# Storing the last group's two larger chunks in two transfers each, in a 1x1 depthwise-separable convolution

## The chip, the cores and the metric

The kernel runs on one core of one Trainium2 chip. The metric is the device time of one execution in microseconds (us), as the median of several runs. A profiled run also gives the span: the time from the first to the last of the program's own instructions, some 1.7 us shorter than the device time here.

The **tail** is the time from the end of the last matmul to the end of the span, and the **head** is what lies before the kernel's steady pitch begins. The last matmul's end is read from the trace's record of that instruction.

## The reference

The kernel size is 1, so the depthwise step is a scale of each channel and the whole thing is one matrix product with a scaled weight.

```python
H = W = 384; C = 384; k = 1
x  : (1, H, W, C) bf16     dw : (1, 1, C) bf16     pw : (C, C) bf16

def reference(x, dw, pw):
    ...                       # for k = 1: out = x * dw[0, 0]
    return jnp.einsum('bhwc,cd->bhwd', out, pw)
```

147,456 rows of 384 channels go in and as many come out: 113 MB each way.

## The kernel before

The rows are cut into 288 supertiles of 512 rows. For each, VectorE transposes the input (two instructions), TensorE multiplies it with the scaled weight (48 matmuls into one of two halves of PSUM), and ScalarE copies the result from PSUM into an output buffer in one instruction. SyncE issues all stores and nearly all loads. Supertiles are loaded and stored in chunks; the chunks are small at both ends (comments in the code cuts are this document's; an assert is cut):

```python
NR = 3          # input and output buffers, used in turn by the groups
def _groups(n_super):
    head, tail = [[1, 1, 2, 2, 4]], [[6, 4], [4, 2, 1, 1]]
    mid = n_super - sum(map(sum, head + tail))
    return head + [[LMAX]] * (mid // LMAX) + tail      # LMAX = 10
```

So the last group is four supertiles in one chunk, two in one chunk, and two single ones. A store waits until the chunk's last supertile has been emptied out of PSUM:

```python
def store(t):
    g, i, off, first, L = chunks[t]
    je = first + L - 1
    src = Os[g % NR][:, 4 * off * D : 4 * (off + L) * D]
    rows = of[512 * first : 512 * (first + L), :]
    if first + LONG < NS:                  # all but the last two supertiles
        dst = rows.rearrange("(q p j) d -> p q (j d)", q=4, p=P)
        src = src.rearrange("p (q e) -> p q e", q=4)
    else:
        dst = rows.rearrange("(m q) d -> m (q d)", q=4)
    if je + 1 == NS:                       # the last supertile: two halves
        for k in range(2):
            part = slice(2 * D * k, 2 * D * k + 2 * D)
            nc.sync.wait_ge(s_a[je % 2], je // 2 + 2 + k)
            nc.sync.wait_ge(s_d, k + 1)
            nc.sync.dma_start(dst[:, part], src[:, part]).then_inc(s_o[g % NR], 16)
        return
    nc.sync.wait_ge(s_a[je % 2], je // 2 + 2)
    nc.sync.dma_start(dst, src).then_inc(s_o[g % NR], 16)
```

The last supertile alone is emptied by ScalarE and VectorE together, a quarter each in turn, so that its first half can be stored earlier:

```python
for q in (0, 2):
    nc.scalar.copy(Ov[:, q, j, :], PS[s][:, q, :D]).then_inc(s_a[s])
    nc.vector.tensor_copy(Ov[:, q + 1, j, :], PS[s][:, q + 1, :D]).then_inc(s_d)
```

At the very end SyncE waits until all stores have landed.

## Time and profile before

| | before |
|---|---|
| median of the first 3 runs | 575.23 us (575.2 to 575.54) |
| span of the profiled run | 573.9 us |
| TensorE busy, share of the span | 567.8 us, 99% |
| VectorE, ScalarE busy | 89%, 73% |
| data moved | 226.88 MB, 395 GB/s |
| end of the last matmul | 569.24 us |
| tail | 4.63 us |

The prediction below shows the lines.

### The profile page before, as it was taken

The page shows a single profiled execution, that of the slowest core. Times are in us where ns is not written, and L with a number is a line of the kernel's source. Part 1 is how long each engine was busy: PE and PEld are TensorE (multiplying, and loading weights), DVE is VectorE, ACT ScalarE, POOL GpSimd, SP SyncE. Part 2 cuts the span into 40 slices and gives each one's busy share as a digit, 9 for nine tenths or more (in the row PEclk, how much of TensorE's full clock was granted, in tenths as well). Part 3 has the DMA queues.
Part 4 walks back from the last instruction along what each step waited for, and adds up shares of the span by engine and source line. Part 5 has one row for each costly group of instructions (what it writes and reads, how often), then busy time and mean ns, then how long its engine had stood idle before and what let it go on. Part 6 is the DMA issues. An engine that isn't in the chain of part 4 may idle for free.

```text
span 573.9 us, 29721 instructions
## 1 busy us (share of the span) xinstructions
PE 567.8 (99%) x13869; PEld 383.5 (67%) x13869; DVE 508.0 (89%) x584; ACT 419.1 (73%) x297; POOL 0.9 (0%) x8
## 2 busy tenths in 40 slices
PE   8999999999999999999999999999999999999996
PEld 4666666666666666666666666666666666666664
DVE  7888988988898898889889888988988898898884
ACT  6777777777777777777777777777777777777775
POOL 0000000000000000000000000000000000000000
PEclk9999999999999999999999999999999999999999
DMA  8999999999999999999999999999999999999676
GB/s 358 441 340 422 427 417 435 430 432 421 412 404 414 389 393 418 407 399 397 435 390 399 398 427 399 393 414 417 403 390 430 400 389 397 419 403 369 266 286 234
DMA packets 25396, 226.88 MB, mean 395 GB/s; under 512 B 1193, under 2 KB 5418, under 8 KB 21546
## 3 DMA queue, kind: packets, MB, share of 16 engines
q1 hardware_dynamic: 24208, 225.61, 97.1%
q10 hardware_dynamic: 1178, 1.18, 0.6%
q14 instruction: 9, 0.07, 0.0%
q8 instruction: 1, 0.02, 0.0%
HBM read 113.54 MB, written 113.25 MB: 395 GB/s over the span
## 4 chain that ended last, share of the span: by engine, by line
PE 99%; DVE 0%; issue 0%; POOL 0%; POOLq 0%; DVEq 0%; SPq 0%
PE ps L189 98%; PE ps L239 1%; PE ps L206 0%; DVE O L330 0%; POOL zero L255 0%; POOL warm L254 0%; PE ps L221 0%; POOLq L365 0%; DVEq L326 0%; SPq L103 0%
## 5 line engine op out<-in xcount | busy, mean ns | idle before, releaser
L189 PE MATMUL ps<-w_r,T 32*128 32x384 bf16 x13824 | 562.2, 321 | 0.0
L282 DVE STREAM_TRANSPOSE T<-X 128x384 uint32<-128x384 uint32 x572 | 501.2, 877 | 55.4 <-DMA X<-in_x_dram 0.2
L332 ACT CAST O<-ps 128x1536 bf16<-128x1536 f32 x287 | 413.0, 1439 | 147.5 <-PE ps L189 147.5
L189 PEld LDWEIGHTS ps<-w_r,T 32*128 32x128 bf16 x13824 | 381.5, 93 | 181.0 <-issue 0.7
L295 ACT CAST w_r<-ps 128x768 bf16<-128x768 f32 x5 | 3.7, 805 | 1.1 <-PE ps L239 1.0
L206 PE MATMUL ps<-zero 32*128 32x384 bf16 x24 | 2.6, 494 | 1.4 <-POOL zero L255 1.4
L282 DVE STREAM_TRANSPOSE T<-Xl 128x384 uint32<-128x384 uint32 x4 | 3.5, 878 | 0.4
L330 DVE CAST O<-ps 128x384 bf16<-128x384 f32 x2 | 1.0, 553 | 3.1 <-PE ps L189 3.1
L239 PE MATMUL ps<-pw_n,sel_w 64*128 64x384 bf16 x18 | 3.1, 521 | 0.0
L267 ACT ACT_TABLE_LOAD x1 | 1.3, 1283 | 1.9 <-issue 1.9
L206 PEld LDWEIGHTS ps<-zero 32*128 32x128 bf16 x24 | 0.7, 99 | 2.6 <-issue 2.6
L239 PEld LDWEIGHTS ps<-pw_n,sel_w 64*128 64x128 bf16 x18 | 1.2, 139 | 1.5 <-issue 1.2
L300 DVE TENSOR_REDUCE sel<-eye 128x64 f32<-128x128 bf16 x1 | 0.3, 289 | 1.8 <-POOL eye L257 1.8
L295 DVE CAST w_r<-ps 128x768 bf16<-128x768 f32 x1 | 1.0, 957 | 0.9 <-PE ps L239 0.9
L329 ACT CAST O<-ps 128x384 bf16<-128x384 f32 x2 | 0.9, 482 | 0.5 <-PE ps L189 0.5
L310 DVE TENSOR_SCALAR sel_w<-sel,dw_f 128x256 bf16<-128x256 f32 x3 | 0.9, 351 | 0.0
L307 DVE COPY dw_f<-ps 128x3 f32<-128x3 f32 x1 | 0.2, 161 | 0.8 <-PE ps L221 0.8
L221 PEld LDWEIGHTS ps<-ones,dw_row 1*128 1x128 bf16 x3 | 0.2, 101 | 0.2 <-issue 0.2
L257 POOL TENSOR_SCALAR_AFFINE_SELECT eye<-ones 128x128 bf16<-128x128 bf16 x1 | 0.3, 295 | 0.1
L267 ACT COPY warm<-warm 128x1 f32<-128x1 f32 x2 | 0.3, 190 | 0.0
L255 POOL MEMSET zero<- 128x192 uint32 x1 | 0.3, 258 | 0.0
L221 PE MATMUL ps<-ones,dw_row 1*128 1x1 bf16 x3 | 0.2, 161 | 0.0
(6 smaller groups left out, 0.7 us busy)
## 6 DMA issues: line engine op xcount, KB each, us to landing
X<-in_x_dram SPq DMA_DIRECT2D x26, 3840.0 KB, 21.0
out_dram<-O SPq DMA_DIRECT2D x26, 3840.0 KB, 26.8
X<-in_x_dram SPq DMA_DIRECT2D x3, 1536.0 KB, 17.0
out_dram<-O SPq DMA_DIRECT2D x3, 1536.0 KB, 6.9
X<-in_x_dram SPq DMA_DIRECT2D x3, 768.0 KB, 8.3
out_dram<-O SPq DMA_DIRECT2D x3, 768.0 KB, 14.3
X<-in_x_dram SPq DMA_DIRECT2D x1, 2304.0 KB, 18.6
out_dram<-O SPq DMA_DIRECT2D x1, 2304.0 KB, 10.5
```

The lines of the kernel that those rows point to most:

```text
L189: mm = nc.tensor.matmul(PS[s][:, q, :D], lhsT=Ts[s][32 * q : 32 * q + 32, b, par::2], rhs=w_r[32 * q : 32 * q + 32, b, par, :], start=(b, ...
L206: nc.tensor.matmul(PS[0][:, i, :D], lhsT=zero[32 * i : 32 * i + 32, 0:P], rhs=zero[32 * i : 32 * i + 32, :], start=True, stop=True, tile_p ...
L221: mm = nc.tensor.matmul(PS[1][:, 0, D + k : D + k + 1], lhsT=dw_row[:, P * k : P * k + P], rhs=ones[0:1, 0:1], start=True, stop=True,)
L239: mm = nc.tensor.matmul(PS[(k + 1) % 2][:, 2 * r + v, :D], lhsT=sel_w[64 * v : 64 * v + 64, k, r, :, :].rearrange("p q w -> p (q w)"), rhs ...
L255: nc.gpsimd.memset(zero[:].bitcast(U32), 0).then_inc(s_zero)
L267: c = nc.scalar.copy(warm[:, s + 1 : s + 2], warm[:, 0:1])
L282: ins = nc.vector.transpose(out=Tw[:, 3 * h : 3 * h + 3], in_=Xw[:, :, j, 96 * h : 96 * h + 96].rearrange("p k (b w) -> p b k w", w=32),)
L295: o = nc.vector.tensor_copy(out, in_) if e == 0 else nc.scalar.copy(out, in_)
L310: nc.vector.tensor_scalar_mul(sel_w[:, k], sel[:].unsqueeze(2).to_broadcast([P, 2, 4, 32]), dw_f[:, k : k + 1]).then_inc(s_sw)
L329: nc.scalar.copy(Ov[:, q, j, :], PS[s][:, q, :D]).then_inc(s_a[s])
L330: nc.vector.tensor_copy(Ov[:, q + 1, j, :], PS[s][:, q + 1, :D]).then_inc(s_d)
L332: a = nc.scalar.copy(Ov[:, :, j, :], PS[s][:, :, :D])
```

## The change

Its intent is to start the last group's big stores earlier, so that they don't stand in front of the small last ones. The chunks of four and of two are each stored in two transfers, each issued when its part has been emptied.

```diff
+    n_parts = [2 if c[0] + 1 == len(groups) and (c[4] > 1 or c[3] + 1 == NS) else 1 for c in chunks]
...
-        def store(t):
-            je = first + L - 1
+        def store(t, k):
+            je = first + L * (k + 1) // n_parts[t] - 1
...
                 src = src.rearrange("p (q e) -> p q e", q=4)
+                e = L * D // n_parts[t]
+                dst, src = dst[:, :, e * k : e * k + e], src[:, :, e * k : e * k + e]
...
-            todo.append((first + L + 1, store, t))
+            for k in range(n_parts[t]):
+                todo.append((first + L * (k + 1) // n_parts[t] + 1, store, (t, k)))
...
-            n = sum(map(len, groups[o::NR])) + ((len(groups) - 1) % NR == o)
+            n = sum(n_parts[t] for t, c in enumerate(chunks) if c[0] % NR == o)
```

Cut: the last supertile's two halves take the new argument `k` in place of their own loop, and do what they did; `todo` holds tuples of arguments.

More of the change, by code (lines that the diff above doesn't have):

```diff
@@ L133, in store @@
                 src = src.rearrange("p (q e) -> p q e", q=4)
+                e = L * D // n_parts[t]
+                dst, src = dst[:, :, e * k : e * k + e], src[:, :, e * k : e * k + e]
             else:
                 dst = rows.rearrange("(m q) d -> m (q d)", q=4)
-            if je + 1 == NS:
-                for k in range(2):
-                    part = slice(2 * D * k, 2 * D * k + 2 * D)
-                    nc.sync.wait_ge(s_a[je % 2], je // 2 + 2 + k)
-                    nc.sync.wait_ge(s_d, k + 1)
-                    nc.sync.dma_start(dst[:, part], src[:, part]).then_inc(s_o[g % NR], 16)
+            if first + 1 == NS:
+                je = first
+                part = slice(2 * D * k, 2 * D * k + 2 * D)
+                nc.sync.wait_ge(s_a[je % 2], je // 2 + 2 + k)
+                nc.sync.wait_ge(s_d, k + 1)
+                nc.sync.dma_start(dst[:, part], src[:, part]).then_inc(s_o[g % NR], 16)
                 return
@@ L153 @@
             if 0 < t < NT - LONG:
-                todo.append((g_end[g - NR] if g >= NR else -1, load_x, t))
-            todo.append((first + L + 1, store, t))
-        for _, f, t in sorted(todo, key=lambda a: a[0]):
-            if f is store and t == 0:
+                todo.append((g_end[g - NR] if g >= NR else -1, load_x, (t,)))
+            for k in range(n_parts[t]):
+                todo.append((first + L * (k + 1) // n_parts[t] + 1, store, (t, k)))
+        for _, f, a in sorted(todo, key=lambda a: a[0]):
+            if f is store and a[0] == 0:
                 for _ in range(28):
                     nc.sync.wait_ge(s_pw, 16)
-            f(t)
+            f(*a)
         for o in range(NR):
-            n = sum(map(len, groups[o::NR])) + ((len(groups) - 1) % NR == o)
+            n = sum(n_parts[t] for t, c in enumerate(chunks) if c[0] % NR == o)
             nc.sync.wait_ge(s_o[o], 16 * n)
```

## The prediction

> **What bounds the kernel now.** I read the page's busy shares first, then the chain of work that ended last, then the end of the span microsecond by microsecond, then the store queue's timeline and its packets. The chain, in order of time:
>
> ```profile
> 7.05 562.22 PE ps L189 x13824
> 569.26 0.03 issue
> 569.29 0.02 DVEq L326
> 569.31 0.04 issue
> 569.36 1.02 DVE O L330 x2
> ```
>
> TensorE alone sets the time from 7.05 us to 569.26 us: 13,824 matmuls back to back, 98% of the span. The granted clock is 1.00 all the way. The change touches no matmul, so at most what lies behind 569.26 us can move. The span ends at 573.86 us (573.9 on the page), so that is 4.6 us, 0.8% of the time.
>
> What fills these 4.6 us? The chain stops at 570.38 us, with the last copy out of PSUM; what follows is transfers, which the chain doesn't follow. The table by stage, one row a microsecond (columns: PE, weight load, VectorE, ScalarE, GpSimd busy, clock, DMA share, GB/s):
>
> ```profile
> 562.00:563.00 1.00, 1.00 (x32) 0.68 (x28) 0.90 (x2) 0.93 (x1) 0.00 (x0) 1.00 0.00 0
> 563.00:564.00 1.00, 1.00 (x32) 0.66 (x24) 0.90 (x2) 0.56 (x1) 0.00 (x0) 1.00 0.16 61
> 564.00:565.00 1.00, 1.00 (x33) 0.66 (x25) 0.90 (x2) 0.88 (x1) 0.00 (x0) 1.00 1.01 402
> ...
> 570.00:571.00 1.00, 0.00 (x0) 0.00 (x0) 0.38 (x1) 0.15 (x1) 0.00 (x0) 1.00 1.00 390
> 571.00:572.00 1.00, 0.00 (x0) 0.00 (x0) 0.00 (x0) 0.00 (x0) 0.00 (x0) 1.00 1.01 367
> 572.00:573.00 1.00, 0.00 (x0) 0.00 (x0) 0.00 (x0) 0.00 (x0) 0.00 (x0) 1.00 0.05 15
> ```
>
> The DMA engines move nothing in 562 to 563 us and are then full, without a hole, until just after 572 us. So the tail has a backlog of stores that begins late. Who begins it is seen in the store queue's timeline (start, length, line; read in single stretches):
>
> ```profile
> 555.15 0.37 SPq L144 DMA_DIRECT2D out_dram<-O  x1
> 562.95 0.37 SPq L144 DMA_DIRECT2D out_dram<-O  x1
> 566.85 2.29 SPq L144 DMA_DIRECT2D out_dram<-O  x2
> 568.80 0.34 SPq L144 DMA_DIRECT2D out_dram<-O  x1
> 570.00 0.85 SPq L141 DMA_DIRECT2D out_dram<-O  x2
> ```
>
> These are the stores of the group before's last chunk (4 supertiles), then of the last group: 4 supertiles (1536 KB), 2 (768 KB, at 566.85), 1 (384 KB, at 568.80) and the last one in two halves of 192 KB (570.00 and 570.46). With 1.573 + 0.786 + 0.393 + 0.393 = 3.146 MB at some 380 GB/s they need 8.3 us, and by the packet records they run from 563.85 to 572.16 us. The last store lands at 572.54 us, SyncE's wait for it ends at 572.56 us, and 1.30 us of closing semaphores and drains follow to 573.86 us.
>
> **What the Trainium skill says, and whether the trace agrees.** (1) DMA: Bandwidth & Descriptors, section "Queues, rings and completion order": on each DMA engine descriptors are consumed in ring order. The trace agrees: the first 1536-byte packet of the 2-supertile store starts at 567.85 us, just as the 3072-byte packets of the store before run out (567.97 us), though it was issued at 566.85. A late big store thus delays the small last ones. (2) Same page, "Latency and other measured facts": first byte some 600 ns after issue on the sync and scalar path. The trace differs: where the engines had room, the first packet came 0.90 us after the issue's start (547.35 to 548.25, 555.15 to 556.05, 562.95 to 563.85); I use 0.90. (3) Same page, "Anatomy of one DMA": a fixed cost of about 2 us, mostly the receipt of the write. Stated for GpSimd's path; the last two stores here took 2.0 and 2.1 us with 0.53 us of packets in each, and from the last packet's end to the landing it is 0.38 us only. (4) Same page, "Why small descriptors are slow (HBM only)": each packet has a small fixed overhead. The trace lets it be measured, below.
>
> **The change part by part.** It removes no byte and adds two store issues: the 4-supertile store becomes two of 768 KB, issued after its second and its fourth supertile is emptied; the 2-supertile store becomes two of 384 KB. The instruction lists of TensorE, VectorE, ScalarE and GpSimd stay the same.
>
> *Issue times.* One copy out of PSUM ends each supertile, every 1.95 us:
>
> ```profile
> 557.59 1.44 ACT L332 CAST O<-ps 128x1536 bf16<-128x1536 f32 x1 [0.51 <-PE ps L189]
> 559.54 1.44 ACT L332 CAST O<-ps 128x1536 bf16<-128x1536 f32 x1 [0.51 <-PE ps L189]
> 561.49 1.44 ACT L332 CAST O<-ps 128x1536 bf16<-128x1536 f32 x1 [0.51 <-PE ps L189]
> ```
>
> The store at 562.95 follows the copy that ends at 562.93, so 561.49 is the chunk's fourth supertile and 557.59 its second. Part A of the four can go at 559.05, part B stays at 562.95. Of the two, part A goes at 562.95 + 1.95 = 564.90 and part B stays at 566.85. SyncE sits idle at both new times; an issue takes it 0.37 us.
>
> *Packet times.* 128 partitions over 16 engines are 8 packets an engine for each contiguous piece. The share of queue 1 in 564.2 to 567.6 us (3072-byte packets only) and in 568.2 to 569.8 us (1536-byte only), and of queue 10 in 34 to 38 us (768-byte packets of another transfer):
>
> ```profile
> q1 hardware_dynamic: 440, 1.35, 102.8%
> ...
> q1 hardware_dynamic: 384, 0.59, 101.6%
> ...
> q10 hardware_dynamic: 225, 0.17, 12.7%
> ```
>
> 3.4 us x 16 x 1.028 / 440 = 127 ns; 1.6 x 16 x 1.016 / 384 = 68 ns; 4 x 16 x 0.127 / 225 = 36 ns. That is about 6 ns a packet plus 0.039 ns a byte. Four supertiles whole: 32 packets x 127 ns = 4.06 us; in halves 2 x 32 x 67 ns = 4.29 us. Two supertiles whole: 32 x 67 = 2.14 us; in halves 2 x 32 x 36 = 2.30 us. The split costs 0.39 us of DMA time in all, but 2.14 us of it is moved into the hole before 563.85 us.
>
> *The queue replayed.* A part starts at its issue + 0.90 us or when the part before it is through:
> - 4A: 559.95, but the chunk before holds 15 engines until 560.17 and one, which lags, until 561.50. Through at 562.3, on the laggard at about 563.7: before 4B in both cases.
> - 4B: 563.85 to 565.99. 2A: ready 565.80, so 565.99 to 567.14.
> - 2B: 567.75 to 568.90: here the backlog is gone for the first time.
> - Single supertile: 569.70, 8 x 127 ns, to 570.72. Last supertile, first half: 570.90 to 571.43 (8 x 67 ns). Second half: ready 571.36, so 571.43 to 571.97.
>
> Check on before: the same rule gives 563.85 + 4.06 + 2.14 + 1.02 + 0.54 + 0.54 = 572.15, against 572.16 in the records. So the last packet ends 0.2 us earlier, and landing and closing follow unchanged: the span should be about 573.66 us. Without a hole for the last half, the limit is that its data is there only at 570.46 us: 0.90 + 0.54 + 0.38 later is 572.28 us, so 0.26 us is all the gain that these latencies leave, whatever is done to the earlier stores. Median 575.23 - 0.2 = 575.0 us. That is 0.04%, far below the 2% mark.
>
> **The rivals.**
> - *The issue latency takes the backlog's place, but is smaller.* The stores of the last two supertiles have one contiguous piece a partition, not four. Both were hidden behind the backlog, so 0.90 us is shown only for the four-piece form. With the skill's 0.6 us the last landing would be at 570.46 + 0.6 + 0.54 + 0.38 = 571.98, a gain of 0.56 us: 574.7 us. Against it: a load at the start with one piece a partition, issued at 1.54 us, first moved at 2.95 us, no sooner than the stores[...].
> - *The split eats its own gain.* If packets of 768 bytes in a store cost more than the 36 ns read off a load, 2B has 0.80 us of slack before the single supertile (568.90 to 569.70), so up to 61 ns a packet stays hidden. If descriptors came too slowly or the laggard engine held 4A past 563.85, 4B could start later, by a few tenths. Then the gain is 0 to 0.1 us: 575.2 us.
> - *The transfer is hidden anyway.* If the closing waited for something else, nothing would move. SyncE's wait for the stores ended 0.02 us after the last landing, which speaks against it: chance small.
> - *TensorE gets slower* as stores lie beside matmuls from 560 to 562 us. Stores lie beside them now (564 to 569 us) with the same 32 matmuls a microsecond. Nothing.
>
> **Range and chances.** The gain has a middle of 0.2 us and lies between 0 and 0.56 us by the rivals. The three runs of before lie 0.34 us apart (575.2 to 575.54), as large as the gain, and a median of such runs moves by some 0.15 us. Low: 575.2 - 0.56 is 574.64, so 574.6. High: no gain and a median 0.2 us up, 575.4. A difference of 2% is 11.5 us, more than twice what lies behind the last matmul, so faster by 2% could not come from the change; slower by 2% would need TensorE to stall. 0.99 for within 2%.
>
> **What would show it right or wrong.** In the changed trace: store issues at 559.05 and 564.90 besides the old ones; DMA share near full in 560.2 to 562.3 us; 4B still first moving at 563.85 us; 768-byte packets of 36 ns; a first hole in the DMA share between about 568.9 and 569.7 us; the last packet's end near 572.0 and the landing near 572.33 us; the last half 1.9 us from issue to landing in place of 2.08. Wrong would be: no hole before the single supertile (then packet cost), or the single store's packets starting less than 0.90 us after 568.80 (then the first rival), or a chain whose matmuls end at another time than 569.26 us.

## The result, and the profile after

The changed kernel took 575.19 us in the median of 6 runs (575.01 to 575.78); the kernel before, in 6 runs that include the first three, 575.29 us (575.15 to 575.81). The ratio is the mean time of one kernel's fast runs over that of the other's of the same rounds, so it isn't quite the ratio of these medians: 0.9998, with a 95% interval of 0.9985 to 1.0011.

The span of the profiled run fell from 573.9 to 573.3 us, 0.59 us, more than the medians did. Two stages made that, and only one has to do with the change.

**The head.** The first copy of a supertile out of PSUM, in the timelines of ScalarE, before and then after (start, length, line; in brackets the idle time before it):

```profile
9.64 1.44 ACT L332 CAST O<-ps 128x1536 bf16<-128x1536 f32 x1 [1.33 <-PE ps L189]
```

```profile
9.15 1.44 ACT L336 CAST O<-ps 128x1536 bf16<-128x1536 f32 x1 [0.92 <-PE ps L193]
```

It comes 0.48 us earlier after, and by the records so do all 289 of ScalarE's copies, each by 0.481 or 0.482 us: both kernels keep a pitch of 1.95 us from the first supertile to the last. So 0.48 of the 0.59 us were won before 10 us, where both programs are the same. The stage of the product's first matmuls says how (TensorE alone; columns: busy with the number of matmuls, clock, DMA share, GB/s), before and then after:

```profile
7.00:8.00 1.00, 0.95 (x16) 1.00 1.02 412
8.00:9.00 1.00, 1.00 (x32) 1.00 1.03 424
```

```profile
7.00:8.00 1.00, 1.00 (x28) 1.00 1.01 418
8.00:9.00 1.00, 1.00 (x32) 1.00 1.01 418
```

The full rate is 32 matmuls a microsecond. Before, the first twelve ran at about half of it: in the records the groups of four start 0.27 to 0.32 us apart and then 0.163 us. After, they start 0.163 to 0.173 us apart from the first group on. The matmuls that fold the scale into the weight, just before, show the same halving: their pairs start 0.32 us apart and then 0.163 us, from 5.6 us on after, and not at all before. The three slow groups cost 0.42 us, and the product's first matmul began 0.07 us later as well. The Trainium skill has it: TensorE: Matmul & The Clock Gate, section "What's actually happening", says that the array starts at half clock, that a short window of activity releases it, and that this window runs freely, so that the point of release differs from run to run. The trace agrees in the factor of two and in the scatter (below), though the clock column shows 1.00 throughout. This difference belongs to the run, not to the kernel.

**The tail.** It fell from 4.63 to 4.52 us, by 0.11 us. The store queue's timeline of the changed kernel, read in single stretches:

```profile
558.57 0.37 SPq L147 DMA_DIRECT2D out_dram<-O  x1
562.47 0.37 SPq L147 DMA_DIRECT2D out_dram<-O  x1
564.42 0.37 SPq L147 DMA_DIRECT2D out_dram<-O  x1
566.37 0.37 SPq L147 DMA_DIRECT2D out_dram<-O  x1
568.32 0.34 SPq L147 DMA_DIRECT2D out_dram<-O  x1
569.52 0.82 SPq L144 DMA_DIRECT2D out_dram<-O  x2
```

All old issues stand where they stood, 0.48 us earlier (562.95 is now 562.47, 570.00 is 569.52), and the new ones at 558.57 and 564.42 are 0.48 us before the predicted 559.05 and 564.90. The stages of the changed kernel, with the columns of the prediction's table:

```profile
559.00:560.00 1.00, 1.00 (x35) 0.74 (x28) 0.88 (x1) 0.94 (x1) 0.00 (x0) 1.00 1.00 363
560.00:561.00 1.00, 1.00 (x32) 0.74 (x28) 0.88 (x1) 0.49 (x1) 0.00 (x0) 1.00 1.01 370
561.00:562.00 1.00, 1.00 (x32) 0.74 (x28) 0.90 (x2) 0.99 (x1) 0.00 (x0) 1.00 0.76 267
...
568.00:569.00 1.00, 0.76 (x20) 0.28 (x12) 0.13 (x1) 0.49 (x2) 0.00 (x0) 1.00 0.51 167
569.00:570.00 1.00, 0.00 (x0) 0.00 (x0) 0.90 (x2) 0.66 (x2) 0.00 (x0) 1.00 0.85 335
570.00:571.00 1.00, 0.00 (x0) 0.00 (x0) 0.00 (x0) 0.00 (x0) 0.00 (x0) 1.00 0.79 286
571.00:572.00 1.00, 0.00 (x0) 0.00 (x0) 0.00 (x0) 0.00 (x0) 0.00 (x0) 1.00 0.46 166
```

The idle stretch of before is now full up to 561.8 us, and the DMA share has holes after 568 us, where before it was 1.00 until 572 us. The backlog is gone. What the last two stores gained by it is small; the line for their way from issue to landing, before and then after:

```profile
DMA to landing us min/median/max: 2.0/2.0/2.1
```

```profile
DMA to landing us min/median/max: 1.9/1.9/2.0
```

By the records the last one took 2.08 us before and 1.97 us after, and these 0.11 us are the whole of the tail's change.

**A trap in the page.** The chain of the changed kernel ends like this:

```profile
564.88 0.02 issue
564.90 1.45 ACT O L336
566.35 0.02 issue
566.37 2.51 DMA out_dram<-O
568.88 1.01 DVE O L334 x2
```

It says that VectorE's last copies waited for the landing of a store, and TensorE's share falls from 98% to 97% by it. That is not so. VectorE does check that semaphore, but for the stores of earlier groups in the same buffer, which had long landed. The semaphore is shared with the new part, whose landing happened to come close to the moment when the copy began, and the inference took it for the releaser. VectorE's copy starts 0.12 us after the end of the last matmul in both kernels, so TensorE released it in both. By the records the last of the new part's 16 increments came 0.23 us after that matmul, when the copy had begun already.

### The profile page after: what moved, and what is told of

Read it like the earlier page. It is cut to its first block, busy times and chain, and to the rows that moved or that the text cites. A ratio compares the mean times of both kernels' runs of the same rounds, so it can differ in the third digit from the quotient of the medians.

```text
span 573.3 us, 29723 instructions
## 1 busy us (share of the span) xinstructions
PE 566.7 (99%) x13869; PEld 411.9 (72%) x13869; DVE 507.4 (89%) x584; ACT 419.0 (73%) x297; POOL 0.9 (0%) x8
## 4 chain that ended last, share of the span: by engine, by line
PE 97%; DMA 1%; ACT 1%; DVE 0%; issue 0%; SPq 0%
PE ps L193 97%; DMA pw_n<-in_pw_dram 1%; DMA out_dram<-O 0%; ACT w_r L299 0%; ACT O L336 0%; DVE O L334 0%; PE ps L243 0%; SPq L369 0%; SPq L104 0%
## 5 line engine op out<-in xcount | busy, mean ns | idle before, releaser
L193 PE MATMUL ps<-w_r,T 32*128 32x384 bf16 x13824 | 561.8, 321 | 0.5 <-ACT w_r L299 0.5
L193 PEld LDWEIGHTS ps<-w_r,T 32*128 32x128 bf16 x13824 | 410.0, 93 | 152.3 <-issue 0.9
```

What stands on the lines that cost most here:

```text
L193: mm = nc.tensor.matmul(PS[s][:, q, :D], lhsT=Ts[s][32 * q : 32 * q + 32, b, par::2], rhs=w_r[32 * q : 32 * q + 32, b, par, :], start=(b, ...
```

## The experiments

Eight runs were made, six of them of new kernels, all but two with correct results. Since the head scatters by more than the effect, they are judged by the tail. Single runs on one core have the state "unknown"; times are compared only in the two cases that ran in several rounds.

**1. Both kernels once more: `rep_before` and `rep_after`** (no edit). How well does a tail repeat?

> The kernel before once more, to learn how well a profile repeats. The tail (from the end of the last matmul to the end of the span) was 4.63 us before and 4.52 us after the change; the head (up to where the copies out of PSUM settle at a pitch of 1.95 us) differed by 0.48 us the other way round of what the change could do. If the tail is set by the stores as I think, it comes out at 4.63 +- 0.03 us again, while the span may differ by some 0.5 us. If the tail scatters by 0.1 us too, the change's 0.11 us is not shown by one profile.

> The changed kernel once more. If the 0.11 us of tail is the change's own, the tail is 4.52 +- 0.03 us again; if it was scatter, it may come out near 4.63 us. The head is expected to differ from run to run whatever the kernel.

Measured: tails of 4.63 us (`rep_before`) and 4.52 us (`rep_after`), as in the first pair. Tails repeat to 0.01 us, so 0.11 us is clear of scatter. The spans went the other way: 573.6 us for the kernel before and 573.9 us for the changed one. The reason is in the head again: against the first profile of before, the copies came 0.32 us earlier in `rep_before` and 0.14 us later in `rep_after`. Over all ten profiles that shift covers 0.76 us, seven times the change's effect. Two things make it, by the records: the matmuls reach their full rate between 5.6 us (`after`) and 8.2 us (`six3`), which costs the product's first groups up to 0.5 us, and the first matmul on the loaded weight starts between 3.96 and 4.21 us. A comparison of medians could not have shown the 0.11 us.

**2. One split at a time: `only4` and `only2`.**

```diff
-    ... (c[4] > 1 or c[3] + 1 == NS) ...
+    ... (c[4] == 4 or c[3] + 1 == NS) ...     # only4
+    ... (c[4] == 2 or c[3] + 1 == NS) ...     # only2
```

> Only the four-supertile chunk is stored in two parts; the two-supertile chunk goes whole. Replay, in us from the end of the last matmul: second part of the four done at -3.1, the chunk of two (issued -2.39) moves from -1.49 to 0.78, the single supertile to 1.80, the halves of the last to 2.34 and 2.88 on the engine that is last. So the last packet ends at 2.88, against 2.92 before and 2.81 after: tail about 4.59 us. If instead moving the four's first half into the idle stretch is all that counts, the tail equals the changed kernel's, 4.52.

> Only the two-supertile chunk is stored in two parts; the four goes whole and late as before. Replay: the four moves from -5.4 to -1.2, the halves of the two follow with 32 packets of 38 ns each, to 1.2, the single to 2.2, the last halves to 2.8 and 3.3. So the last packet ends near 3.2 us against 2.92 before: tail about 4.9 us, 0.25 us longer than before. If any split of a late store helps by itself, the tail is at or below 4.63 us.

Measured: tails of 4.55 us and of 4.95 us. For `only4` that is neither the expected 4.59 us nor the 4.52 us of the alternative: the chunk of four alone wins 0.08 of the 0.11 us. The replay was right in kind: the single supertile's packets start 0.64 us after the last matmul, just as those of the chunk of two run out, where with both splits they start at 0.40 us. Its last packet came at 2.85 us, 0.03 us sooner than replayed. The chunk of two alone loses 0.31 us against before. The last two stores of `only2` from issue to landing:

```profile
DMA to landing us min/median/max: 2.3/2.4/2.4
```

Splitting a store that stands in a full queue only adds packets: in `only2` the 768-byte packets took 39 ns each, so that 64 of them an engine last 2.5 us where 32 of 1536 bytes last 2.1 us. In these runs a split helps by what it moves into idle time; a gain of another kind does not show.

**3. The size of the backlog: `six1` and `six3`.** The last group's chunks are 6, 1 and 1, and the six is stored whole, or in three parts.

```diff
-    ... tail = [[1, 1, 2, 2, 4]], [[6, 4], [4, 2, 1, 1]]
+    ... tail = [[1, 1, 2, 2, 4]], [[6, 4], [6, 1, 1]]
-    n_parts = [2 if c[0] + 1 == len(groups) and (c[4] > 1 or c[3] + 1 == NS) else 1 for c in chunks]
+    n_parts = [1 if c[0] + 1 == len(groups) and c[4] == 6 else 2 if c[3] + 1 == NS else 1 for c in chunks]   # six1
+    n_parts = [3 if c[0] + 1 == len(groups) and c[4] == 6 else 2 if c[3] + 1 == NS else 1 for c in chunks]   # six3
```

> The last group's chunks are 6, 1 and 1 and the six is stored whole, at -2.39 us. If the backlog of late stores sets the end, 32 packets of 184 ns run from -1.49 to 4.4 us, the single to 5.4, the last halves to 6.5 us: tail about 8.2 us, 3.6 us longer than before, and the median some 3.6 us over before's (0.6%). If the end is set by the last store's own latency and the stores before it are hidden, the tail stays at 4.6 us.

> Chunks 6, 1 and 1 with the six stored in three parts of two supertiles, each when emptied. From the parts on this is the same queue as the kernel that splits the four alone: last packet near 2.88 us, tail 4.59 us (+- 0.05), so that the split is worth 3.6 us here where it is worth 0.1 us in the change. If splitting itself had a gain or a cost of its own, it would show here as a tail off 4.59 us.

Measured: tails of 8.14 us and of 4.51 us. The times, in 4 runs each: 578.76 us (578.69 to 578.81) for `six1`, a ratio of 1.0061 to before (1.0044 to 1.0078), and 575.23 us for `six3`, a ratio of 0.9998 (0.9981 to 1.0015). In `six1` the stages after the last matmul (at 568.93 us) are full of transfer:

```profile
572.00:573.00 1.00, 0.00 (x0) 0.00 (x0) 0.00 (x0) 0.00 (x0) 0.00 (x0) 1.00 1.00 401
573.00:574.00 1.00, 0.00 (x0) 0.00 (x0) 0.00 (x0) 0.00 (x0) 0.00 (x0) 0.67 1.02 399
574.00:575.00 1.00, 0.00 (x0) 0.00 (x0) 0.00 (x0) 0.00 (x0) 0.00 (x0) 0.50 1.01 366
575.00:576.00 1.00, 0.00 (x0) 0.00 (x0) 0.00 (x0) 0.00 (x0) 0.00 (x0) 0.50 0.30 105
```

So a late store sets the end as the replay says, and the same kind of split is worth 3.6 us of tail here. The expectation for `six3` was missed by 0.08 us, more than its 0.05: the last packet came at 2.84 us, not 2.88, and landed 0.35 us later, not 0.38 (0.35 us in `six1` too). Why the landing is shorter with these chunks isn't tested. The split is worth 0.11 us in the change because the kernel before had nearly no backlog left to take away: its last supertile's first half moved its first packet 0.94 us after its issue, against 0.84 us in the changed kernel, so the queue was only 0.1 us behind.

**4. Nothing ahead of the last stores: `no_big` and `half_only`.** Their outputs are wrong, which doesn't matter for the times.

```diff
+    n_parts = [2 if c[3] + 1 == NS else 0 if c[0] + 1 == len(groups) and c[4] > 1 else 1 for c in chunks]  # no_big: four and two not stored
+    n_parts = [2 if c[3] + 1 == NS else 0 if c[0] + 1 == len(groups) else 1 for c in chunks]               # half_only: and the single not,
+            for k in range(first + 1 == NS, n_parts[t]):                                                   # nor the last one's first half
```

Cut: in `half_only` the wait at the end counts one store for the last supertile.

> Wrong on purpose: the chunks of four and of two of the last group are not stored at all, so nothing stands ahead of the last two supertiles. If the changed kernel's tail is limited by its last supertiles' own issue, latency and packets, the tail stays at 4.52 us (+- 0.03). If the small early parts still hold it back, it falls by 0.1 us or more.

> Wrong on purpose: of the last group only the second half of the last supertile is stored. This is the floor of one store: issue at 1.22 us after the last matmul, first packets 0.84 us later on the first engine and some 0.13 us later on the last one, 8 packets x 67 ns, 0.38 us to the landing, 1.33 us of closing: tail 1.22 + 0.84 + 0.13 + 0.54 + 0.38 + 1.33 = 4.44 us, 0.08 us under the changed kernel. If the latency falls when nothing else is on the way (0.6 us to the first packet), the tail is near 4.2 us and there would be more to win by an earlier start of the other stores.

Measured: tails of 4.53 us and of 4.44 us. With the six supertiles' stores taken away altogether the tail is the changed kernel's (4.52 us) within 0.01 us: the change has taken all that was to be had from these stores. With a single half store left on empty DMA engines it takes 1.89 us from issue to landing, against 1.97 us in the changed kernel; the first packet starts 0.84 us after the issue, so the latency doesn't fall when nothing else moves. Of the difference of 0.08 us, 0.07 lies before the landing. I read it as the price of the last supertile's first half, which is still on the engines when the second half is ready; the single supertile is left out too, but in the changed kernel its packets end at 1.53 us, before the first half's start at 1.60.

**5. A shorter last copy: `balanced`** (not run).

```diff
-    nc.scalar.copy(Ov[:, q, j, :], PS[s][:, q, :D])
-    nc.vector.tensor_copy(Ov[:, q + 1, j, :], PS[s][:, q + 1, :D])
+    nc.scalar.copy(Ov[:, q : q + 2, j, :224], PS[s][:, q : q + 2, :224])
+    nc.vector.tensor_copy(Ov[:, q : q + 2, j, 224:], PS[s][:, q : q + 2, 224:D])
```

Cut: the semaphore increments at the ends of these lines.

> The changed kernel, with the last supertile's copies shared 448 to 320 columns a half between ScalarE and VectorE in place of 384 to 384 (ScalarE ended at 0.91 us, VectorE at 1.14 us after the last matmul). By the copies' durations (ScalarE 0.48 us for 384 and 1.44 us for 1536 elements, VectorE 0.55 us for 384 and 0.96 us for 768) both should end at about 1.01 us, the two last issues move to about 0.69 and 1.10 us, the first half's packets start at 1.53 and the second half follows them directly: last packet 2.74 in place of 2.81 us, tail 4.45 in place of 4.52 us. If the two engines disturb each other when they read the same part of PSUM at once, the copies grow longer than that and the tail is 4.52 us or more.

The check before the chip refused it as a race: ScalarE and VectorE would read the same bank of PSUM with nothing to order them. So whether a better share of the last copies would win the 0.07 us is open. No experiment points to a version that beats the changed kernel by more than these hundredths.

All tails on one table (last matmul to the end of the span; last packet's end and last landing from the records, from the same zero):

| kernel | last packet | landing | tail | expected tail |
|---|---|---|---|---|
| before, repeated | 2.92, 2.92 | 3.30, 3.31 | 4.63, 4.63 | 4.63 |
| after, repeated | 2.81, 2.82 | 3.19, 3.19 | 4.52, 4.52 | 4.42 (prediction), 4.52 |
| only the four split | 2.85 | 3.23 | 4.55 | 4.59 |
| only the two split | 3.26 | 3.62 | 4.95 | 4.9 |
| 6, 1, 1 whole | 6.47 | 6.82 | 8.14 | 8.2 |
| 6, 1, 1 in three | 2.84 | 3.19 | 4.51 | 4.59 |
| four and two not stored | 2.80 | 3.20 | 4.53 | 4.52 |
| second half alone | 2.74 | 3.12 | 4.44 | 4.44 |

## Why the prediction was right or wrong

- **The bound.** Right. TensorE's stream kept its pitch in all ten profiles, and only the tail could move. The measured median of 575.19 us lies in the range, near the predicted 575.0 us, and "within 2%" had been given a chance of 0.99. But the median can't confirm the 0.2 us: the heads alone scatter by 0.76 us.
- **The issue times and the idle stretch.** Right to the hundredth of a microsecond, once the run's 0.48 us are taken off.
- **The queue replayed.** Right in kind: the backlog was gone after the chunk of two, and a hole came before the single supertile (in the first profile's records from 0.14 us before the last matmul's end to 0.40 us after it). It was not the first hole, as the prediction's list of signs has it: in its own replay 2A ends at 567.14 and 2B starts at 567.75, and the records have that hole too, from 1.73 to 1.49 us before the last matmul's end.
- **The signs of being wrong.** Two of the three came up. The single supertile's packets started 0.84 us after its issue, less than 0.90: that is the first rival, at 0.06 us in place of the 0.30 us that it had. And the matmuls ended at 568.76 us, which is the run's head and not the change.
- **The size.** This step was mis-sized: 0.2 us in the prediction, 0.11 us by the tails. The term that failed is "A part starts at its issue + 0.90 us", for all 16 engines at once. The one-piece stores start at 0.84 us on the first engine, and the engines finish over 0.15 us: the first half's sixteen completion packets start 1.37 to 1.52 us after its issue, where the replay had all packets done at 1.43. The landing counts the last engine. On it the first half starts near 0.98 us after its issue (1.52 less 8 packets of 67 ns), and two halves follow each other: the last packet ended 1.59 us after the second half's issue, against 1.51 us in the prediction.
- **Why the check on before didn't catch this.** Two errors cancelled. I multiplied counts by durations (127 and 67 ns), yet the shares of 102.8% and 101.6% say that the packets of one engine overlap: 3.4 us x 16 / 440 is one every 123.6 ns, and 1.6 x 16 / 384 one every 66.7 ns. Over the 88 packets of an engine that made the replayed backlog 0.15 us too long: 32 x 123.6 + 32 x 66.7 + 8 x 123.6 + 16 x 66.7 ns = 8.15 us in place of 8.30. The engines' spread of 0.15 us was missing. In the long queue of before they balance; in the short one of after the spread is left.
- **The rival of a smaller latency.** Wrong in its size: 0.84 us, not 0.6 us, and 0.84 us again with empty engines. The floor of one store, with the issue times as they are, is a tail of 4.44 us, so at most 0.19 us was to be had, not 0.26.
- **The rival of dearer packets.** The 768-byte packets took 38 ns, not 36, and the holes hid it.
- **The rival of the laggard engine.** It was there, and I had it too early. I put the end of the four's first part on that engine at 563.7 us of before's time, 5.5 us before the last matmul's end. By the records it ended 5.0 and 4.5 us before it in the two profiles: later than the second part's start at 5.4 us before it. The holes swallowed the delay; before the single supertile 0.5 us were left in one profile and 0.4 us in the other. Why one engine trails is not tested and stays open.
- **TensorE beside stores, and a transfer hidden anyway.** Neither came true; the pitch stayed and the tail moved with the last landing.

## What to carry to other kernels

Splitting a late store is worth the time that it moves into an idle stretch of the DMA engines, up to the moment when the last store's own data, latency and packets take over; replay the queue before you edit, and look first for the idle stretch. The Trainium skill's advice in Perfetto Trace Analysis, section "DMA Optimizations", puts the condition more widely: splitting may help where the DMA engines are generally idle. Here they were busy for 97% of the span, and a hole of some 3.7 us near the end was enough. The split gave 0.11 us or 3.6 us, or cost 0.31 us, depending on the backlog. When an effect is smaller than a run's scatter, measure it from an event behind the scattered stage, such as the last matmul.

## What the Trainium skill lacked or had wrong

- DMA: Bandwidth & Descriptors, "Latency and other measured facts", gives some 600 ns to the first byte on the sync path. Here the first packet of a store started 0.84 us (one piece a partition) or 0.90 us (four pieces) after the start of the issue, 0.84 us also in `half_only`, where no other store was near, and the 16 engines finished a small store over 0.15 us.
- The same page, "Anatomy of one DMA", has a fixed cost of about 2 us, for GpSimd's path. A lone 192 KB store from SyncE took 1.89 us in all, 0.38 us of it from the last packet's end to the landing.
- The same page has no figure for how far the packets of one engine overlap: here the busy share of a saturated stretch was 102.8%, with packets of 127 ns one every 123.6 ns.
- No page that I read gives a figure for an issue into a long queue: in the kernel with the six stored whole SyncE's last issue took 1.19 us, against 0.34 to 0.40 us for the same issue in the other kernels. That the queue's length made it so isn't tested.
